# Attention feeding a squared-ReLU MoE: which side of a PSUM copy is strided, and in which order the first loads run

## The chip, the cores and the metric

One core of a Trainium2 chip runs the whole program in one launch. The metric is the device time in microseconds. TensorE (PE) multiplies, VectorE (DVE), ScalarE (ACT) and GpSimd (POOL) work element by element, SyncE (SP) and POOL issue DMAs; all five run their own instruction streams in order and wait for each other by semaphores.

## The reference

Attention over 8 batch rows, 8 heads, 576 positions, head size 64. Heads 0 to 3 see a sliding window of 32 positions, heads 4 to 7 every fourth position of the last 128. The attention output, as 4608 tokens of 512 values, goes through an expansion to 2048, a squared ReLU and a projection back.

```python
rel = pos[:, None] - pos[None, :]
mask_plain = (rel >= 0) & (rel < 32)
mask_dil = (rel >= 0) & (rel < 128) & (rel % 4 == 0)
scores = np.where(masks, scale * (q @ k.T), -1e9)
attn = softmax(scores)
x = (attn @ v).transpose(0, 2, 1, 3).reshape(4608, 512)
h = x @ w_in                  # 512 x 2048
out = np.maximum(h, 0.0) ** 2 @ w_out   # 2048 x 512
```

Inputs and output are float32; the kernel works in fp16 with fp32 sums.

## The kernel before

The program alternates two kinds of work. **Attention** (`attn`) takes one batch row at a time, 8 in all. **MoE** (`moe_gen`) takes chunks of 512 tokens, 9 in all. `moe_gen(c)` is a generator that yields after every two matmuls or so, 64 times in all, and `pump(n)` runs it n yields further. From batch row 1 on, `attn(b, ...)` calls `pump(gap)` between its steps with a gap of 3, so that chunk b-1 fills the holes of row b; what is left of the chunk is pumped at the row's end. After row 7 chunks 7 and 8 run alone.

One row of attention, by the names that profile and text use:

- The loads. q and k of the sliding heads come as fp32 into `sq`, v as fp32 into `sv` (sliding, six DMAs) and `sd` (dilated, two DMAs), all on SP's queue. q and k of the dilated heads come already cast to fp16 into `nd`, on POOL's queue. A DMA from POOL can cast, and the weights `wi` and `wo` (4 DMAs of 512 KB each, counted as fp16) come that way too. `sq`, `sv` and `sd` have one buffer, `nq` and `nd` two.
- Casts: `sq` to `nq`, `sv` to `vp`, `sd` to `vd`. For row 0 DVE casts `nq`, POOL `vp` and ACT `vd`; later rows cast all on POOL.
- `t_sliding` (two calls per row) transposes `nq` on PE into the PSUM tile `pt`, 12 transposes of 96 columns; then DVE copies the half of k and ACT the half of q into `QKTp`. `t_dilated` does the same from `nd` by `pd` to `QKTd`, with two copies on each engine. A row of q was loaded as groups of 6 (or 12) neighbouring positions in one partition, so the transposes leave position 6p+j at column 96j+p, and the copies put the positions in order.
- `s_sliding` and `s_dilated` compute scores into `ps` and `pz`, ACT takes the exponential into `AT`, DVE multiplies by a mask.
- `av_sliding` and `av_dilated` compute `pav` and `paw`; DVE divides by the sum (RECIPROCAL, then x_p or x_d). `x_sliding` and `x_dilated` transpose the result into `px` and `py`, and DVE copies them into `xT`, the input of the MoE.

All these PSUM tiles (pt, pd, ps, pz, pav, paw, px, py) share **two** buffers of one pool: pd can start only when pt's buffer has been emptied by DVE and ACT, the second ps only when pd's has. In a MoE chunk `ph` is the PSUM tile of the expansion (16 per chunk, 4 matmuls each), ACT takes the ReLU (`rt`), DVE squares it (`g`), and `po` is the tile of the projection (4 per chunk, 16 matmuls each), copied by ACT into `ot` and stored by SP. ph and po share four further buffers.

The instruction order on each engine follows the code, with shifts by the Tile framework's scheduler, which moves an instruction ahead where its inputs come earlier; the order within an engine is then fixed. Before the loop the program issues the loads of row 0 and `wi`, then casts, the loads of row 1, the attention of row 0 without any MoE work, and `wo`. L129 and L131 are the lines of `copy`, one helper for all the copies and casts named above: `scalar.copy` on ACT, `tensor_copy` on DVE and POOL.

Of the kernel before, what the change touches and what calls it, by code (L numbers as in the profile page):

```python
# [9 lines left out]
FP32 = mybir.dt.float32  # L10
I16 = mybir.dt.int16
ALU = mybir.AluOpType
ACTF = mybir.ActivationFunctionType
P = 128
# [3 lines left out]
def kernel(  # L18
# [9 lines left out]
    nc = tc.nc  # L28

    B, H, S, D = q.shape  # L30
    W = 32
    DIL = 4
# [13 lines left out]
    QB = 96  # L46
    NB = S // QB
    PADP = P - QB
    CL = S // DIL
    QD = CL // 2  # L50
    PADD = P - QD
    UW = 576

    const = ctx.enter_context(tc.tile_pool(name="const", bufs=1))
# [51 lines left out]
        return nd  # L106

    def load_w_in():
        for j in range(4):
            nc.gpsimd.dma_start(  # L110
                out=wi[:, :, 512 * j : 512 * (j + 1)],
                in_=moe_w_in[:, 512 * j : 512 * (j + 1)].rearrange(
                    "(dh dl) f -> dl dh f", dl=P
                ),
            )

    def load_w_out():
        for j in range(4):
            nc.gpsimd.dma_start(
                out=wo[:, 4 * j : 4 * (j + 1), :],  # L120
                in_=moe_w_out[4 * j * P : 4 * (j + 1) * P, :].rearrange(
                    "(fh fl) m -> fl fh m", fl=P
                ),
            )


    def copy(eng, o, i):
        if eng is nc.scalar:
            nc.scalar.copy(o, i)  # L129
        else:  # L130
            eng.tensor_copy(o, i)  # L131
# [12 lines left out]

    def cast_v(engs):
        for m in range(0, NB, 2):
            copy(engs[0], vp[:, m : m + 2, :, 0:D], sv[:, m : m + 2, :, :])
        for t in range(2):
            for c in range(0, DIL, 2):
                copy(  # L150
                    engs[1],
                    vd[:, t, c : c + 2, :, 0:D],
                    sd[:, t, :, D * c : D * (c + 2)].rearrange("p h (c d) -> p c h d", d=D),
                )
# [4 lines left out]
    nc.vector.memset(sv[0:PADP, 0, :, :], 0.0)  # L159
    nc.vector.memset(sd[0:64, 0, :, :], 0.0)  # L160
    load_v(0)
    load_w_in()

    make_identity(nc, ident)
    reli = const.tile([P, QB], I16, name="reli")
# [33 lines left out]
    def moe_gen(c):  # L199
        g = gp.tile([P, NFF, TOKC], FP16, name=f"g{c}", tag="g")  # L200
        for ffc in range(NFF):
            ph = pmool.tile([P, TOKC], FP32, name=f"ph{c}_{ffc}", tag="pm")
            for dmk in range(NDM):
                nc.tensor.matmul(  # L204
                    ph,
                    wi[:, dmk, ffc * P : ffc * P + P],
                    xT[:, dmk, c * TOKC : (c + 1) * TOKC],
                    start=(dmk == 0),
                    stop=(dmk == NDM - 1),
                )  # L210
                if dmk == 1:
                    yield
            rt = osb.tile([P, TOKC], FP16, name=f"rt{c}_{ffc}", tag="rt")
            nc.scalar.activation(rt, ph[:], ACTF.Relu)  # L214
            nc.vector.tensor_mul(g[:, ffc, :], rt, rt)  # L215
            yield
        for t in range(TOKC // P):
            po = pmool.tile([P, DM], FP32, name=f"po{c}_{t}", tag="pm")
            for ffc in range(NFF):
                nc.tensor.matmul(  # L220
                    po,
                    g[:, ffc, t * P : (t + 1) * P],
                    wo[:, ffc, :],
                    start=(ffc == 0),
                    stop=(ffc == NFF - 1),
                )
# [24 lines left out]
    def t_sliding(b, n, hp):  # L251
        pt = pa(f"pt{b}_{hp}", FP16)
        for i in (1, 0):
            for j in range(6):
                nc.tensor.transpose(  # L255
                    pt[:, i, QB * j : QB * (j + 1)],
                    n[:, i, j, 2 * hp : 2 * hp + 2, :],
                    ident[0:QB, 0:QB],
                )
        for i, eng in ((1, nc.vector), (0, nc.scalar)):  # L260
            copy(
                eng,
                QKTp[:, i, hp, PADP:].rearrange("x (p j) -> x j p", j=6),
                pt[:, i, 0:UW].rearrange("x (j p) -> x j p", p=QB),
            )

    def t_dilated(b, n, g):
        pt = pa(f"pd{b}_{g}", FP16)
        for i in (1, 0):
            for j in range(6):  # L270
                nc.tensor.transpose(  # L271
                    pt[:, i, QB * j : QB * (j + 1)],
                    n[:, i, g, P * j : P * (j + 1)],
                    ident[0:QB, 0:QB],
                )
        for i, eng in ((1, nc.vector), (0, nc.scalar)):
            for h in range(2):
                copy(
                    eng,
                    QKTd[:, i, 2 * g + h, :, PADD:].rearrange("x a (p s) -> x a s p", s=3),  # L280
                    pt[:, i, 0:UW].rearrange("x (s a h p) -> x a h s p", a=2, h=2, p=48)[
                        :, :, h
                    ],
                )
# [99 lines left out]
    def x_dilated(b, t, xs):  # L384
        py = pa(f"py{b}_{t}", FP16)
        for a in range(2):
            for e in range(2):
                x = xs[a][:, e].rearrange("p h d -> p (h d)")
                for c in range(2):
                    o = 288 * c + QD * (2 * a + e)  # L390
                    nc.tensor.transpose(  # L391
                        py[:, 0, o : o + QD],
                        x[0:QD, P * c : P * (c + 1)],
                        ident[0:QD, 0:QD],
                    )
        t0 = b * S + 288 * t
        nc.vector.tensor_copy(  # L397
            xT[:, 2:4, t0 : t0 + 288].rearrange("x c (i r) -> x c r i", r=DIL),
            py[:, 0, 0:UW].rearrange("x (c r i) -> x c r i", c=2, r=DIL),
        )  # L400

    def attn(b, nq, nd, gap):
        t_sliding(b, nq, 0)
        pump(gap)
        t_sliding(b, nq, 1)
        pump(gap)
        t_dilated(b, nd, 0)
        pump(gap)
        s_sliding(b, 0)
        pump(gap)  # L410
        t_dilated(b, nd, 1)
        pump(gap)
        s_sliding(b, 1)
        pump(gap + 2)
        s_dilated(b, 0)
        pump(gap + 2)
        s_dilated(b, 1)
        pump(gap + 1)
        xs = []
        for mp in range(3):  # L420
            xs.append(av_sliding(b, mp))
            pump(gap)
            if mp == 1:
                x_sliding(b, 0, xs)
# [12 lines left out]
        pump(gap)  # L437
        x_dilated(b, 1, zs)

    nq = cast_sliding_qk(0, (nc.vector, nc.vector))  # L440
    cast_v((nc.gpsimd, nc.scalar))
    load_sliding_qk(1)
    load_v(1)
    attn(0, nq, nds[0], 0)
    nds[1] = load_dilated_qk(1)
    load_w_out()
    nxt = 0
    for b in range(1, B):
        pending.append(moe_gen(b - 1))
        pump(1)  # L450
        nq = cast_sliding_qk(b, (nc.gpsimd, nc.gpsimd))
        cast_v((nc.gpsimd, nc.gpsimd))
        if b + 1 < B:
            load_sliding_qk(b + 1)
            load_v(b + 1)
            nds[b + 1] = load_dilated_qk(b + 1)
        attn(b, nq, nds[b], 3)
        pump(1000)
    for c in range(B - 1, NTOKC):
        pending.append(moe_gen(c))  # L460
# [31 lines left out]
```

## Time and profile before

| | |
|---|---|
| time, median of 2 runs | 399.22 us (399.0 to 399.44) |
| the profiled execution's own time | 401.02 us |
| its span, first to last instruction | 399.2 us |
| PE busy | 328.8 us (82%) |
| DVE, ACT, POOL busy | 227.0, 186.4, 80.8 us |
| granted PE clock, mean of the span | 0.970 |
| HBM read and written | 39.85 and 9.44 MB |

Lines of the profile read "line, engine, operation, output <- input, shapes, count", then busy time and mean ns of one, then how long the engine stood idle before the group and what ended the wait. A timeline row has start and length in us first. A stretch row (from:to) has the length, then busy us and count for PE, PE's weight loads, DVE, ACT and POOL, the granted clock, the DMA share and GB/s. A row of a DMA queue has packets, MB and the time of its packets as a share of 16 engines over the stretch.

### The profile page before, as it was taken

Reading aid. Unit: us, or ns where it says so; the run is one execution under the profiler, and the core shown is the slowest. Engines: PE = TensorE matmul, PEld = TensorE weight load, DVE = VectorE, ACT = ScalarE, POOL = GpSimd, SP = SyncE. Lnnn points to the kernel's source line nnn. Section 1 sums busy time; section 2 is a strip of 40 time slices with the busy share of each in tenths; the row PEclk is TensorE's granted clock in tenths of the full one; section 3 lists DMA queues with packets and bytes.
Section 4 is the critical chain, followed back from the end, with each engine's and each line's share of the span. In section 5 each row is a group of like instructions: output and inputs, shape, how many; then the busy total and the mean of one; then the engine's idle time right before and its main releaser. Section 6 shows DMA issues by size and latency. Waiting matters only on the chain.

```text
span 399.2 us, 6698 instructions
## 1 busy us (share of the span) xinstructions
PE 328.8 (82%) x2656; PEld 170.0 (43%) x2656; DVE 227.0 (57%) x420; ACT 186.4 (47%) x297; POOL 80.8 (20%) x127
## 2 busy tenths in 40 slices
PE   0203677999699969996999699969996999999995
PEld 0102443455345524552455345534553455444442
DVE  4603787757575666666665666566666666420410
ACT  0018327812791188218821773178317841642721
POOL 6045045162222132313231322100210000000000
PEclk9999998999899989999899989998999899999999
DMA  8999999978434454445344033400010001001002
GB/s 179 196 219 209 196 221 193 182 161 236 121 59 116 148 120 62 103 162 118 62 103 136 27 59 95 145 27 2 29 53 28 0 13 69 26 27 68 12 29 80
DMA packets 50368, 40.81 MB, mean 102 GB/s; under 512 B 26016, under 2 KB 45728, under 8 KB 50336
## 3 DMA queue, kind: packets, MB, share of 16 engines
q1 hardware_dynamic: 42528, 31.46, 32.2%
q0 software_dynamic: 7808, 8.92, 13.8%
q8 instruction: 21, 0.34, 0.3%
q14 instruction: 11, 0.09, 0.1%
HBM read 39.85 MB, written 9.44 MB: 123 GB/s over the span
## 4 chain that ended last, share of the span: by engine, by line
PE 68%; ACT 12%; DVE 11%; DMA 5%; issue 2%; SPq 0%; ACTq 0%
PE po L220 31%; PE ph L204 26%; ACT QKTp L129 6%; DVE QKTp L131 4%; DMA sd<-in_v_dram 3%; ACT QKTd L129 3%; DVE QKTd L131 2%; ACT rt L214 2%; PE pd L271 2%; PE paw L358 2%; DMA sq<-in_k_dram 2%; PE pav L344 1%; PE pz L315 1%; PE ps L297 1%; DVE g L215 1%
## 5 line engine op out<-in xcount | busy, mean ns | idle before, releaser
L204 PE MATMUL ph<-xT,wi 128*128 128x512 f16 x576 | 149.2, 400 | 0.1
L220 PE MATMUL po<-wo,g 128*128 128x512 f16 x576 | 137.2, 379 | 0.0
L214 ACT ACTIVATE rt<-ph 128x512 f16<-128x512 f32 x144 | 87.6, 624 | 42.6 <-PE ph L204 42.2
L215 DVE TENSOR_TENSOR g<-rt 128x512 f16<-128x512 f16 x144 | 67.0, 465 | 66.3 <-ACT rt L214 63.7
L230 ACT COPY ot<-po 128x512 f32<-128x512 f32 x36 | 21.1, 586 | 121.6 <-PE po L220 118.2
L204 PEld LDWEIGHTS <-wi 128*128 128x128 f16 x576 | 52.9, 102 | 56.6 <-issue 7.4
L220 PEld LDWEIGHTS <-g 128*128 128x128 f16 x576 | 51.7, 98 | 51.7
L271 PE MATMUL pd<-ident,nd 96*128 96x96 f16 x192 | 14.9, 246 | 31.0 <-ACT QKTp L129 30.4
L131 DVE COPY QKTp<-pt 128x576 f16<-128x576 f16 x16 | 33.0, 2080 | 7.4 <-PE pt L255 7.4
L131 POOL CAST vp<-sv 128x512 f16<-128x512 f32 x24 | 15.3, 641 | 105.8 <-PE pav L344 41.7
L129 ACT COPY QKTp<-pt 128x576 f16<-128x576 f16 x16 | 33.1, 2094 | 7.4 <-DVE QKTp L131 7.4
L131 POOL CAST nq<-sq 96x768 f16<-96x768 f32 x28 | 23.7, 882 | 41.8 <-PE pt L255 27.7
L131 DVE COPY QKTd<-pd 128x288 f16<-128x288 f16 x32 | 18.0, 634 | 22.3 <-PE pd L271 22.2
L271 PEld LDWEIGHTS <-nd 96*128 96x128 f16 x192 | 13.8, 122 | 37.5 <-issue 36.1
L297 PE MATMUL ps<-QKTp 64*128 64x96 f16 x192 | 10.6, 218 | 21.5 <-ACT QKTd L129 15.6
L397 DVE COPY xT<-py 128x576 f16<-128x576 f16 x16 | 23.0, 1443 | 6.1 <-PE py L391 5.3
L131 POOL CAST vd<-sd 128x512 f16<-128x512 f32 x28 | 17.3, 624 | 30.2 <-PE paw L358 27.5
L330 DVE TENSOR_TENSOR x_d<-paw,rcp_d 72x512 f16<-72x512 f32 x32 | 22.0, 686 | 1.1
L297 PEld LDWEIGHTS <-QKTp 64*128 64x128 f16 x192 | 7.2, 99 | 34.2 <-issue 30.8
L129 ACT COPY QKTd<-pd 128x288 f16<-128x288 f16 x32 | 17.9, 661 | 7.6 <-DVE QKTd L131 7.5
L255 PE MATMUL pt<-ident,nq 96*128 96x96 f16 x192 | 11.9, 216 | 10.3 <-DVE nq L131 10.3
L287 ACT ACTIVATE AT<-ps 128x576 f16<-128x576 f32 x32 | 19.2, 652 | 1.6 <-PE ps L297 1.6
(46 smaller groups left out, 218.3 us busy)
## 6 DMA issues: line engine op xcount, KB each, us to landing
out_dram<-ot SPq DMA_DIRECT2D x36, 256.0 KB, 2.9
sv<-in_v_dram SPq DMA_DIRECT2D x40, 128.0 KB, 2.8
sq<-in_q_dram SPq DMA_DIRECT2D x8, 576.0 KB, 8.8
sq<-in_k_dram SPq DMA_DIRECT2D x8, 576.0 KB
sd<-in_v_dram SPq DMA_DIRECT2D x8, 512.0 KB
nd<-in_q_dram POOLq DMA_DIRECT2D x16, 144.0 KB, 5.9
nd<-in_k_dram POOLq DMA_DIRECT2D x16, 144.0 KB, 6.3
sd<-in_v_dram SPq DMA_DIRECT2D x8, 288.0 KB
```

The costliest lines, as they stand in the source:

```text
L129: nc.scalar.copy(o, i)
L131: eng.tensor_copy(o, i)
L204: nc.tensor.matmul(ph, wi[:, dmk, ffc * P : ffc * P + P], xT[:, dmk, c * TOKC : (c + 1) * TOKC], start=(dmk == 0), stop=(dmk == NDM - 1),)
L214: nc.scalar.activation(rt, ph[:], ACTF.Relu)
L215: nc.vector.tensor_mul(g[:, ffc, :], rt, rt)
L220: nc.tensor.matmul(po, g[:, ffc, t * P : (t + 1) * P], wo[:, ffc, :], start=(ffc == 0), stop=(ffc == NFF - 1),)
L230: nc.scalar.copy(ot, po)
L271: nc.tensor.transpose(pt[:, i, QB * j : QB * (j + 1)], n[:, i, g, P * j : P * (j + 1)], ident[0:QB, 0:QB],)
L287: nc.scalar.activation(AT[:, u, 0:UW], ps[:, :, 0 : UW // 2], ACTF.Exp, scale=scale)
L297: nc.tensor.matmul(ps[:, e, QB * m3 : QB * (m3 + 1)], QKTp[r, 1, hp, QB * m : QB * m + P], QKTp[r, 0, hp, PADP + QB * m : PADP + QB * (m + ...
L330: nc.vector.tensor_tensor(out=x[0:w], in0=pv[:, :, :, 0:D], in1=rcp[0:w].unsqueeze(3).to_broadcast([w, 2, HH, D]), op=ALU.mult,)
L397: nc.vector.tensor_copy(xT[:, 2:4, t0 : t0 + 288].rearrange("x c (i r) -> x c r i", r=DIL), py[:, 0, 0:UW].rearrange("x (c r i) -> x c r i ...
```

## The change

Two things are changed. The first is the access pattern of the copies that reorder positions: QKTp from pt, QKTd from pd, and xT from py. Before, they read PSUM in its order and write fp16 with a step of 6, 3 and 4 elements; now they read PSUM with a step of 96, 192 and 72 elements and write in order.

```diff
-                QKTp[:, i, hp, PADP:].rearrange("x (p j) -> x j p", j=6),
-                pt[:, i, 0:UW].rearrange("x (j p) -> x j p", p=QB),
+                QKTp[:, i, hp, PADP:].rearrange("x (p j) -> x p j", j=6),
+                pt[:, i, 0:UW].rearrange("x (j p) -> x p j", j=6),
...
-                    QKTd[:, i, 2 * g + h, :, PADD:].rearrange("x a (p s) -> x a s p", s=3),
-                    pt[:, i, 0:UW].rearrange("x (s a h p) -> x a h s p", a=2, h=2, p=48)[
+                    QKTd[:, i, 2 * g + h, :, PADD:].rearrange("x a (p s) -> x a p s", s=3),
+                    pt[:, i, 0:UW].rearrange("x (s a h p) -> x a h p s", a=2, h=2, p=48)[
...
-            xT[:, 2:4, t0 : t0 + 288].rearrange("x c (i r) -> x c r i", r=DIL),
-            py[:, 0, 0:UW].rearrange("x (c r i) -> x c r i", c=2, r=DIL),
+            xT[:, 2:4, t0 : t0 + 288].rearrange("x c (i r) -> x c i r", r=DIL),
+            py[:, 0, 0:UW].rearrange("x (c r i) -> x c i r", c=2, r=DIL),
```

The second is the start of the program. wi is issued (in three DMAs, the last of double size) only behind the vp casts of row 0, wo behind the vd casts, and the loads of row 1 stand in the code behind three small memsets into sq, sv and sd. For row 0 ACT and DVE cast one half of nq each and POOL casts vp and vd. ACT gets a first activation of one column, which loads its table. Chunk 0 starts before row 1's attention, which then runs with a gap of 1.

```diff
     load_v(0)
-    load_w_in()
+    warm = const.tile([P, 1], FP32, name="warm")
+    nc.vector.memset(warm, 0.0)
+    nc.scalar.activation(warm, warm, ACTF.Exp)
...
-    nq = cast_sliding_qk(0, (nc.vector, nc.vector))
-    cast_v((nc.gpsimd, nc.scalar))
+    nq = cast_sliding_qk(0, (nc.scalar, nc.vector))
+    cast_v_sliding()
+    load_w_in()
+    cast_v_dilated()
+    load_w_out()
+    attn(0, nq, nds[0], 0)
+    pending.append(moe_gen(0))
+    pump(1)
+    pump(14)
+
+    nc.vector.memset(sq[:, :, :, 0:1], 0.0)
+    nc.vector.memset(sv[:, 1, :, 0:1], 0.0)
+    nc.vector.memset(sd[:, 1, :, 0:1], 0.0)
     load_sliding_qk(1)
     load_v(1)
-    attn(0, nq, nds[0], 0)
     nds[1] = load_dilated_qk(1)
-    load_w_out()
+    pump(18)
     for b in range(1, B):
-        pending.append(moe_gen(b - 1))
-        pump(1)
+        if b > 1:
+            pending.append(moe_gen(b - 1))
+            pump(1)
...
-        attn(b, nq, nds[b], 3)
+        attn(b, nq, nds[b], 1 if b == 1 else 3)
```

POOL's first casts and DMAs, before (nd_98 is row 0's nd, nd_433 row 1's, nq_446 row 1's nq):

```order
L105 DMA nd_98<-in_q_dram 48x2x768 x2
L105 DMA nd_98<-in_k_dram 48x2x768 x2
L110 DMA wi<-in_moe_w_in_dram 128x4x512 x4
L131 CAST vp<-sv 128x8x64 x3
L105 DMA nd_433<-in_q_dram 48x2x768 x2
L105 DMA nd_433<-in_k_dram 48x2x768 x2
L119 DMA wo<-in_moe_w_out_dram 128x4x512 x4
L131 CAST nq_446<-sq 96x768 x4
```

and after the change (nd_502 and nq_579 are row 1's):

```order
L105 DMA nd_98<-in_q_dram 48x2x768 x2
L105 DMA nd_98<-in_k_dram 48x2x768 x2
L145 CAST vp<-sv 128x8x64 x3
L110 DMA wi<-in_moe_w_in_dram 128x4x512 x2
L110 DMA wi<-in_moe_w_in_dram 128x4x1024
L150 CAST vd<-sd 128x8x64 x4
L117 DMA wo<-in_moe_w_out_dram 128x4x512 x4
L105 DMA nd_502<-in_q_dram 48x2x768 x2
L105 DMA nd_502<-in_k_dram 48x2x768 x2
L129 CAST nq_579<-sq 96x768 x4
```

wi has moved behind the casts of v, and the nd of row 1 has moved behind wo on the same queue.

DVE around the first transposes of row 0, before (nq_140 is row 0's nq, pt_0 and pt_1 its two pt):

```order
L131 CAST nq_140<-sq 96x768 x4
L168 CAST relf<-reli 128x96
L178 TENSOR_TENSOR maskp<-lo__125,hi__126 128x576
L178 TENSOR_TENSOR maskd<-lo__125,hi__126 128x576
L131 COPY QKTp<-pt_0_162 128x6x96
L131 COPY QKTp<-pt_1_177 128x6x96
```

and after:

```order
L129 CAST nq_139<-sq 96x768 x2
L451 MEMSET sq 96x8
L169 CAST relf<-reli 128x96
L179 TENSOR_TENSOR maskp<-lo__124,hi__125 128x576
L452 MEMSET sv 128x4
L179 TENSOR_TENSOR maskd<-lo__124,hi__125 128x576
L129 COPY QKTp<-pt_0_158 128x576
L129 COPY QKTp<-pt_1_173 128x576
```

The scheduler has put two of the three memsets ahead of the copies that empty pt; the third, on sd, stands between the maskp and the maskd products of row 0. The one on sv follows the first vp cast, the one on sd the third vd cast.

ACT where row 1's attention begins, before (rt_0 to rt_3 belong to chunk 0, pt_0 and pt_1 to row 1):

```order
L214 ACTIVATE rt_0_490<-ph_0_443 128x512
L129 COPY QKTp<-pt_0_473 128x6x96
L214 ACTIVATE rt_1_498<-ph_1_493 128x512
L214 ACTIVATE rt_2_521<-ph_2_516 128x512
L129 COPY QKTp<-pt_1_501 128x6x96
```

and after:

```order
L215 ACTIVATE rt_14_565<-ph_14_560 128x512
L215 ACTIVATE rt_15_573<-ph_15_568 128x512
L127 COPY QKTp<-pt_0_606 128x576
L127 COPY QKTp<-pt_1_623 128x576
L288 ACTIVATE AT<-ps_0_0_659 128x576
```

All 16 ph of chunk 0 now stand ahead of row 1's first transposes, and row 1 is mixed with the po of chunk 0. From row 2 on the order on PE, ACT and DVE is nearly that of before.

More of the change, by code (lines that the diff above doesn't have):

```diff
@@ L108, in load_w_in @@
     def load_w_in():
-        for j in range(4):
+        for f0, f1 in ((0, 512), (512, 1024), (1024, 2048)):
             nc.gpsimd.dma_start(
[L111 to L114, printed above, removed]
+                out=wi[:, :, f0:f1],
+                in_=moe_w_in[:, f0:f1].rearrange("(dh dl) f -> dl dh f", dl=P),
             )
@@ L143, in cast_sliding_qk, with cast_v_sliding, cast_v_dilated @@
         return n
-    def cast_v(engs):
+    def cast_v_sliding():
         for m in range(0, NB, 2):
-            copy(engs[0], vp[:, m : m + 2, :, 0:D], sv[:, m : m + 2, :, :])
+            nc.gpsimd.tensor_copy(vp[:, m : m + 2, :, 0:D], sv[:, m : m + 2, :, :])
+    def cast_v_dilated():
         for t in range(2):
             for c in range(0, DIL, 2):
-                copy(
-                    engs[1],
+                nc.gpsimd.tensor_copy(
                     vd[:, t, c : c + 2, :, 0:D],
@@ L438, in attn @@
         x_dilated(b, 1, zs)
-    nq = cast_sliding_qk(0, (nc.vector, nc.vector))
-    cast_v((nc.gpsimd, nc.scalar))
+    nq = cast_sliding_qk(0, (nc.scalar, nc.vector))
[10 more added lines that the diff above has]
+    nc.vector.memset(sd[:, 1, :, 0:1], 0.0)
     load_sliding_qk(1)
     load_v(1)
-    attn(0, nq, nds[0], 0)
     nds[1] = load_dilated_qk(1)
-    load_w_out()
-    nxt = 0
+    pump(18)
     for b in range(1, B):
-        pending.append(moe_gen(b - 1))
-        pump(1)
+        if b > 1:
+            pending.append(moe_gen(b - 1))
+            pump(1)
         nq = cast_sliding_qk(b, (nc.gpsimd, nc.gpsimd))
-        cast_v((nc.gpsimd, nc.gpsimd))
+        cast_v_sliding()
+        cast_v_dilated()
         if b + 1 < B:
```

## The prediction

> **What bounds the kernel now.** I read the page's shares first, then stretches cut where the chain of waits changes its character, then the chain itself.
>
> ```profile
> span 399.2 us, 6698 instructions
> ...
> PE 328.8 (82%) x2656; PEld 170.0 (43%) x2656; DVE 227.0 (57%) x420; ACT 186.4 (47%) x297; POOL 80.8 (20%) x127
> ```
> ```profile
> 0.00:33.60 33.60, 2.29 (x24) 1.94 (x25) 11.15 (x22) 5.44 (x7) 13.68 (x27) 1.00 1.09 200
> 54.90:95.80 40.90, 35.52 (x310) 18.62 (x309) 28.97 (x49) 20.66 (x33) 18.01 (x28) 0.96 1.00 191
> 95.80:136.50 40.70, 36.66 (x317) 19.11 (x316) 26.71 (x48) 21.28 (x34) 10.06 (x15) 0.96 0.47 121
> ```
> TensorE (PE, first number after the length) bounds the whole, but unevenly. In the first 33.6 us it works 2.3 us while the DMA engines (last two numbers: share, GB/s) are full. From 54.9 us each batch row costs some 40.8 us, with about 4 us of PE idle and a mean clock of 0.96.
>
> ```profile
> 94.06 1.73 PE po L220 x8
> ...
> 134.82 1.73 PE po L220 x8
> ...
> 339.73 13.81 PE ph L204 x64
> ...
> 381.17 13.83 PE po L220 x64
> ```
> The chain repeats itself: 134.82 - 94.06 = 40.76 us a row. At the end, with no attention left, 64 matmuls take 13.81 us, 0.216 us each, so a chunk of MoE is 27.6 us. That part can't shrink; the other 13.1 us of a row can. Row 4's PE and one copy, in the timeline:
>
> ```profile
> 180.35 2.10 ACT L129 COPY QKTp<-pt 128x576 f16<-128x576 f16 x1 [1.09 <-DVE QKTp L131]
> 182.50 0.67 PE L271 MATMUL pd<-ident,nd 96*128 96x96 f16 x12 [1.20 <-ACT QKTp L129]
> 184.90 0.30 PE L297 MATMUL ps<-QKTp 64*128 64x96 f16 x6 [0.43 <-ACT QKTp L129]
> 187.96 0.30 PE L297 MATMUL ps<-QKTp 64*128 64x96 f16 x6 [2.22 <-ACT QKTd L129]
> 188.19 1.82 PE L204 MATMUL ph<-xT,wi 128*128 128x512 f16 x4
> 189.81 1.17 PE L271 MATMUL pd<-ident,nd 96*128 96x96 f16 x12
> 190.77 1.93 PE L204 MATMUL ph<-xT,wi 128*128 128x512 f16 x6
> 192.63 0.30 PE L297 MATMUL ps<-QKTp 64*128 64x96 f16 x6
> ```
> PE waits 1.20 + 0.43 + 2.22 = 3.85 us, always for the copy that empties the PSUM buffer it wants next. Then it runs slow: the 4 ph take 1.62 us to the next start instead of 4 x 0.216 = 0.86, the 12 pd 1.17 against the 0.67 of 182.50, the 6 ph 1.86 instead of 1.30. That is 1.8 us more, behind the longest wait alone, where the granted clock falls. Together a row loses **5.6 us** here.
>
> **The copies.** Groups of instructions (mean ns of one before the second bar):
>
> ```profile
> L131 DVE COPY QKTp<-pt 128x576 f16<-128x576 f16 x16 | 33.0, 2080 | 7.4 <-PE pt L255 7.4
> L129 ACT COPY QKTp<-pt 128x576 f16<-128x576 f16 x16 | 33.1, 2094 | 7.4 <-DVE QKTp L131 7.4
> L131 DVE COPY QKTd<-pd 128x288 f16<-128x288 f16 x32 | 18.0, 634 | 22.3 <-PE pd L271 22.2
> L129 ACT COPY QKTd<-pd 128x288 f16<-128x288 f16 x32 | 17.9, 661 | 7.6 <-DVE QKTd L131 7.5
> L397 DVE COPY xT<-py 128x576 f16<-128x576 f16 x16 | 23.0, 1443 | 6.1 <-PE py L391 5.3
> L287 ACT ACTIVATE AT<-ps 128x576 f16<-128x576 f32 x32 | 19.2, 652 | 1.6 <-PE ps L297 1.6
> L330 DVE TENSOR_TENSOR x_p<-pav,rcp_p 96x512 f16<-96x512 f32 x24 | 16.4, 683 | 0.6
> L329 DVE RECIPROCAL rcp_p<-pav 96x8 f32<-96x8 f32 x24 | 4.8, 199 | 7.9 <-PE pav L344 7.9
> L175 DVE TENSOR_SCALAR hi__126<-relf 128x96 f16<-128x96 f32 x1 | 0.2, 203 | 0.0
> L175 DVE TENSOR_SCALAR hi__126<-relf 128x72 f16<-128x72 f32 x1 | 0.2, 190 | 0.0
> ```
> The same 576 elements go from PSUM to contiguous fp16 on ACT in 652 ns (AT<-ps), but to QKTp, whose writes step 12 bytes, in 2094. The steps order the price: 6 bytes (QKTd), 8 (xT from py), 12. So the slow side is the write, and the change takes it away. What the strided read costs, no row shows well. From below: no more than a contiguous read, which on DVE is (683 - 199) / (512 - 8) = 0.96 ns an element over 0.19 us. From above: the RECIPROCAL reads 8 elements 264 bytes apart in 199 ns; the two L175 rows give a fixed part of 203 - 96 x 13 / 24 = 151 ns, so a strided element costs 6.0 ns at most. I take the lower end: in every row above the steps on the write side account for the excess, and x_p, which reads PSUM in broken runs of 64, keeps the plain rate. Then QKTp takes 0.19 + 576 x 0.96 ns = **0.74 us** on DVE and 0.65 on ACT (the AT row), QKTd 0.47 and 0.42 (the same line at 288; for ACT an estimate by its proportion). xT from py falls to 0.74 too; PE has 8 po matmuls to do meanwhile (94.06), so this counts nothing after row 0, and were that cover gone 1.4 us a row.
>
> Row 4 walked again with these numbers. DVE empties pt0 from 178.24 to 178.98; ACT, after its rt, by 179.9; PE wants that buffer for pd0 at 181.1: no wait. pt1 is through both engines by 181.5 and is wanted at 182.9: none. pd0 ends at 181.9; DVE must first do the g of rt2, so its two QKTd copies run 182.4 to 183.3 and ACT's two to 184.1; the second ps wants them at 183.6: **0.5 us** remains, since ACT still starts after DVE. The second pd has the same shape: 0.6. Neither gap is long enough to cost clock (behind the 1.20 us one the 12 pd ran in 0.67). So 1.1 stays of 5.6: **4.5 us a row**, six rows (2 to 7), **27 us**.
>
> **The start.**
>
> ```profile
> 8.85 1.81 DVE L131 CAST nq<-sq 96x768 f16<-96x768 f32 x2 [0.75 <-DMA sq<-in_k_dram]
> ...
> 15.01 0.61 POOL L131 CAST vp<-sv 128x512 f16<-128x512 f32 x1 [7.71 <-DMA sv<-in_v_dram]
> ...
> 28.15 1.28 ACT L129 ACT_TABLE_LOAD   x1 [28.15 <-DMA sd<-in_v_dram]
> ...
> 33.64 1.12 PE L271 MATMUL pd<-ident,nd 96*128 96x96 f16 x12 [21.05 <-ACT QKTp L129]
> ...
> 50.57 1.90 PE L204 MATMUL ph<-xT,wi 128*128 128x512 f16 x4
> ```
> ACT does nothing until sd lands at 28.15, because its first work is the vd casts; its QKTp copies are queued behind, and PE waits for them from 12.6 to 33.64. The vd casts go to POOL and ACT casts q instead (two casts of some 0.9 us from 6.3 on, beside DVE's wait for k, free). DVE's casts of k still end at 10.66, and the transposes near 12.3. The memset on sq is behind them and waits for nothing late. The one on sv stands in DVE's queue **ahead of both QKTp copies** and waits for the first vp cast, now done at 15.6. The DMA queues in two stretches, 12 to 16 us and 28 to 32 us, say how early it can be:
>
> ```profile
> q0 software_dynamic: 624, 0.62, 91.4%
> q1 hardware_dynamic: 631, 0.16, 30.0%
> ```
> ```profile
> q1 hardware_dynamic: 639, 0.92, 108.5%
> q0 software_dynamic: 1, 0.00, 0.2%
> ```
> Beside wi (POOL's queue, q0) the v loads (SP's queue, q1) get packet for packet, 0.16 MB in 4 us; alone q1 moves 0.92. With wi moved behind the vp casts I put the first vp cast's end at 12.5, the last at 14.5, sd at 18 and vd at 20.5. So QKTp is out at 14.8 and pd0 starts there, 19 us sooner. From pd0 to the first ph is 50.57 - 33.64 = 16.9 us; eight QKTd copies on that chain give 1.2 back, so ph begins at 30.5. The memset on sd waits for the third vd cast near 20, the masks that it holds up are due near 23: nothing.
>
> Then the loads. wi is issued at 15; q0 had 1 packet in 28 to 32 although nd was issued at 27, so data flow from 19.5. Its 2.1 MB (four times 512 KB) at 0.62 MB in 4 us are 13.5 us, more while row 1's q and k run beside it: 34.5. The 32 ph up to there are covered by its first half. wo, queued behind, lands at 48, and row 1's nd (four times 144 KB) **behind wo**, at 51.5. PE does its 64 ph by 45.5, then both pt of row 1 and 7 po by 48, and waits 3.5 us for nd. From pd0 on row 1 needs row 0's 16 us, about 2 more for the po between, and 4.5 for py and the last po: chunk 1 starts at **74** instead of 95.8, **21.8 us** sooner. Without the wait it would be 70.5.
>
> Sum: 27 + 21.8 = 48.8. The profiled span of 399.2 becomes 350.4; its own time of 401.02 is 1.8 over that span, and the median of the two runs, 399.22, lies 1.8 below that time, so the median should be **350 us**.
>
> **Rivals.**
>
> *A strided read takes twice the time per element.* For it: no copy here reads PSUM in steps of 144 to 384 bytes, as all of them will. QKTp then takes 0.19 + 576 x 1.92 ns = 1.30 us on DVE and 1.11 on ACT, but QKTd 0.74 and 0.65, longer than the 0.634 of now. The walk gives waits of 2.5 and 1.7 us at the two ps, 4.2 of 5.6; with some clock lost, 1.2 us a row are gained, 7 in all; the start gives 20. 399.2 - 27 = **372 us**. The Trainium skill's page SBUF — State Buffer (section Door 1: The DMA port swizzle) speaks for this: lines of 16 bytes in SBUF that want at least two hits each, of 8 in PSUM, where "any non-contiguous PSUM access pattern significantly slows down matmuls". The write rows above agree with its SBUF half (12-byte steps cost most); of a PSUM read no run here shows it, and by the page the time would be that of this rival.
>
> *The copies gain nothing* (reads as dear as the writes were): the start alone, about 20: **379 us**.
>
> *Row 1's nd and wo take the start back.* The DMA share is still 1.00 in the stretch from 54.9 to 95.8, and row 2's loads press in. If nd lands at 61 instead of 51.5, chunk 1 starts at 83.5: **360 us**, up to 366 if wo is later still.
>
> *Slower than now:* the strided read costs the upper bound, 6.0 ns. QKTp takes 3.6 us on each engine, DVE then ACT: pt0 is out 7.2 us after 178.24, PE wants it after 2.9. The walk gives waits of 4.4, 2.1, 7.6 and 6.4, 20.5 a row, 15 more than now: 6 x 15 = 90 against a start that keeps 10: **480 us**. It decides from about 3.2 ns an element on, where the row's waits reach 9 us, 3.4 more than now, and six rows eat the 20 us of the start. Against it: 8 elements in 199 ns would then all but fill that row.
>
> **How the numbers follow.** Forecast 0.62, double price 0.20, copies gain nothing 0.06, start taken back 0.09, slower 0.03. The forecast's own range is 340 (both 0.5 us waits gone, no wait for nd) to 358. The range for 8 in 10 goes on to the start taken back and the double price: **338 to 375**; the rest is left out. Faster by over 2% (below 391, about what can be told from no change) are all but the last and a tail between: 0.94; same 0.03, slower 0.03.
>
> **What would show it.** QKTp near 0.74 and 0.65 us, QKTd below 0.5; PE's wait of pd for QKTp gone and that of ps for QKTd near 1 us a row; rows of 36.3 us; ACT's first copy before 15 us; pd of row 0 near 15, the first ph near 30, a PE wait for nd near 50, chunk 1 at 74. It is wrong if QKTp stays over 1.2 us, if the memset on sv holds DVE past 16, or if chunk 1 starts after 84.

## The result, and the profile after

The changed kernel takes **355.4 us** (median of two runs, 355.09 to 355.71) against 399.22. The ratio is 0.8902, with a 95% interval of 0.8863 to 0.8942. The profiled execution took 355.09 us, 1.8 more than its span.

The head of the page of the changed kernel, and its groups of copies by shape:

```profile
span 353.3 us, 6704 instructions
...
PE 318.3 (90%) x2656; PEld 164.3 (46%) x2656; DVE 192.2 (54%) x422; ACT 158.9 (45%) x296; POOL 83.2 (24%) x130
```
```profile
L129 DVE COPY QKTp<-pt 128x576 f16<-128x576 f16 x16 | 12.0, 756 | 14.1 <-PE pt L256 14.1
L127 ACT COPY QKTp<-pt 128x576 f16<-128x576 f16 x16 | 10.2, 638 | 11.4 <-DVE QKTp L129 11.3
L129 DVE COPY QKTd<-pd 128x288 f16<-128x288 f16 x32 | 13.0, 448 | 9.2 <-PE pd L272 9.1
L127 ACT COPY QKTd<-pd 128x288 f16<-128x288 f16 x32 | 11.2, 403 | 5.8 <-DVE QKTd L129 5.8
L398 DVE COPY xT<-py 128x576 f16<-128x576 f16 x16 | 12.1, 757 | 9.9 <-PE py L392 9.9
```

DVE and ACT are busy 34.8 and 27.5 us less, PE 10.5 us less, though its number of matmuls is the same: before, it ran part of each row at a lower clock. QKTp went from 2080 and 2094 ns to 756 and 638.

The chain repeats itself in shorter steps, and its end is the old one:

```profile
114.78 1.73 PE po L221 x8
150.43 1.73 PE po L221 x8
...
292.09 1.73 PE po L221 x8
293.81 13.81 PE ph L205 x64
```

Rows 3 to 7 end with the start of the 64 ph: before they took (339.73 - 136.50) / 5 = 40.65 us each, now (293.81 - 116.50) / 5 = 35.46 (116.50 is 114.78 + 1.73, the end of row 2). The stretches of row 2 and row 3, in the columns of the front table's stretch rows:

```profile
78.03:116.50 38.47, 35.61 (x318) 18.41 (x317) 22.83 (x48) 17.58 (x34) 16.30 (x25) 1.00 0.89 217
116.50:152.20 35.70, 35.01 (x318) 18.30 (x316) 22.18 (x48) 17.79 (x34) 10.18 (x15) 1.00 0.52 127
```

Row 3 has PE busy 35.01 of 35.70 us at a full clock. Row 2, which follows the start directly, is 2.8 us longer, with the DMA engines still 0.89 busy. Now PE's timeline, row 0 first, then row 1, the start of chunk 1, two waits of row 2 and the one wait that is left in row 4:

```profile
15.08 1.12 PE L272 MATMUL pd<-ident,nd 96*128 96x96 f16 x12 [2.72 <-ACT QKTp L127]
...
30.15 1.90 PE L205 MATMUL ph<-xT,wi 128*128 128x512 f16 x4
...
57.31 1.12 PE L272 MATMUL pd<-ident,nd 96*128 96x96 f16 x12 [6.85 <-DMA nd<-in_k_dram]
...
78.03 0.59 PE L205 MATMUL ph<-xT,wi 128*128 128x512 f16 x2
...
82.77 0.59 PE L205 MATMUL ph<-xT,wi 128*128 128x512 f16 x2 [0.95 <-ACT ot L231]
...
87.84 0.30 PE L298 MATMUL ps<-QKTp 64*128 64x96 f16 x6 [1.30 <-ACT QKTd L127]
...
159.33 0.30 PE L298 MATMUL ps<-QKTp 64*128 64x96 f16 x6 [0.54 <-ACT QKTd L127]
```

The gain of the span is 45.9 us. Up to the start of chunk 1 it is 95.80 - 78.03 = 17.8 (95.80 is the prediction's mark, the end of chunk 0's last po; chunk 1's first ph began at 95.63); behind it 303.4 becomes 275.3, 28.1: row 2 gives 40.70 - 38.47 = 2.2 and rows 3 to 7 give 5 x 5.19 = 25.9.

### The profile page after: what moved, and what is told of

Same layout as the page of the kernel before. It is cut to its first block, busy times and chain, and to the rows that moved or that the text cites. A ratio compares the mean times of both kernels' runs of the same rounds, so it can differ in the third digit from the quotient of the medians.

```text
span 353.3 us, 6704 instructions
## 1 busy us (share of the span) xinstructions
PE 318.3 (90%) x2656; PEld 164.3 (46%) x2656; DVE 192.2 (54%) x422; ACT 158.9 (45%) x296; POOL 83.2 (24%) x130
## 4 chain that ended last, share of the span: by engine, by line
PE 61%; DMA 16%; ACT 7%; DVE 6%; issue 4%; POOL 2%; SPq 2%; POOLq 0%; ACTq 0%
PE po L221 31%; PE ph L205 22%; DMA sq<-in_k_dram 5%; DMA wi<-in_moe_w_in_dram 4%; DMA sq<-in_q_dram 3%; ACT rt L215 3%; DVE QKTd L129 3%; DVE g L216 2%; DMA sv<-in_v_dram 2%; SPq L92 2%; PE paw L359 2%; DMA out_dram<-ot 2%; ACT QKTd L127 1%; PE pt L256 1%; POOL nq L129 1%
## 5 line engine op out<-in xcount | busy, mean ns | idle before, releaser
L205 PE MATMUL ph<-xT,wi 128*128 128x512 f16 x576 | 139.1, 382 | 2.3 <-ACT rt L215 1.0
L221 PE MATMUL po<-wo,g 128*128 128x512 f16 x576 | 140.1, 381 | 0.0
L129 POOL CAST nq<-sq 96x768 f16<-96x768 f32 x28 | 24.1, 894 | 43.3 <-PE pt L256 20.7
L272 PE MATMUL pd<-ident,nd 96*128 96x96 f16 x192 | 12.1, 219 | 10.2 <-DMA nd<-in_k_dram 6.8
L129 DVE COPY QKTp<-pt 128x576 f16<-128x576 f16 x16 | 12.0, 756 | 14.1 <-PE pt L256 14.1
L288 ACT ACTIVATE AT<-pz 128x576 f16<-128x576 f32 x32 | 19.1, 650 | 0.1
L289 DVE TENSOR_TENSOR AT<-AT,maskp 128x576 f16<-128x576 f16 x32 | 15.0, 468 | 7.5 <-ACT AT L288 5.1
L129 DVE COPY QKTd<-pd 128x288 f16<-128x288 f16 x32 | 13.0, 448 | 9.2 <-PE pd L272 9.1
L398 DVE COPY xT<-py 128x576 f16<-128x576 f16 x16 | 12.1, 757 | 9.9 <-PE py L392 9.9
L256 PEld LDWEIGHTS <-nq 96*128 96x128 f16 x192 | 10.6, 103 | 13.6 <-DVE nq L129 9.6
L289 DVE TENSOR_TENSOR AT<-AT,maskd 128x576 f16<-128x576 f16 x32 | 15.1, 474 | 3.2 <-ACT AT L288 0.3
## 6 DMA issues: line engine op xcount, KB each, us to landing
sq<-in_q_dram SPq DMA_DIRECT2D x8, 576.0 KB, 10.5
```

Source lines behind the costliest of these rows:

```text
L205: nc.tensor.matmul(ph, wi[:, dmk, ffc * P : ffc * P + P], xT[:, dmk, c * TOKC : (c + 1) * TOKC], start=(dmk == 0), stop=(dmk == NDM - 1),)
L221: nc.tensor.matmul(po, g[:, ffc, t * P : (t + 1) * P], wo[:, ffc, :], start=(ffc == 0), stop=(ffc == NFF - 1),)
L256: nc.tensor.transpose(pt[:, i, QB * j : QB * (j + 1)], n[:, i, j, 2 * hp : 2 * hp + 2, :], ident[0:QB, 0:QB],)
L272: nc.tensor.transpose(pt[:, i, QB * j : QB * (j + 1)], n[:, i, g, P * j : P * (j + 1)], ident[0:QB, 0:QB],)
L288: nc.scalar.activation(AT[:, u, 0:UW], ps[:, :, 0 : UW // 2], ACTF.Exp, scale=scale)
L289: nc.vector.tensor_mul(AT[:, u, 0:UW], AT[:, u, 0:UW], mask)
```

## Experiments: the copies

**Each half of the change alone.** First the three new access patterns in the kernel before:

```diff
 # before, start unchanged; QKTp, QKTd and xT as in the change, for example
-                QKTp[:, i, hp, PADP:].rearrange("x (p j) -> x j p", j=6),
-                pt[:, i, 0:UW].rearrange("x (j p) -> x j p", p=QB),
+                QKTp[:, i, hp, PADP:].rearrange("x (p j) -> x p j", j=6),
+                pt[:, i, 0:UW].rearrange("x (j p) -> x p j", j=6),
```

> The three copies of the change in the kernel before, whose start stays. Theory (two separate gains that meet in row 1): rows 2 to 7 give their 28 us, row 1, which here still runs with a gap of 3, some 5, and row 0 some 4, since ACT's two QKTp there end 2.1 us sooner and eight QKTd and two xT copies follow on one chain: 362 us, 358 to 367. Rival (the copies are worth what rows 2 to 7 show and no more, because the start is bound by its loads): 371 us. Rival (half of what rows 2 to 7 gained is owed to the new order at the start): 380 or more.

Measured: 366.2 us (363.9 to 366.4), ratio 0.9167 (0.9134 to 0.9200). The first theory's range holds it, near its upper end: chunk 1 starts at 86.0 and rows 3 to 7 take 35.46 us, but row 2 takes 41.7, with a wait of 4.7 us of ph for ot, which none of the theories had. Then the new start with the three old patterns:

```diff
 # after, start unchanged; QKTp, QKTd and xT as before, for example
-                QKTp[:, i, hp, PADP:].rearrange("x (p j) -> x p j", j=6),
-                pt[:, i, 0:UW].rearrange("x (j p) -> x p j", j=6),
+                QKTp[:, i, hp, PADP:].rearrange("x (p j) -> x j p", j=6),
+                pt[:, i, 0:UW].rearrange("x (j p) -> x j p", p=QB),
```

> The new start with the old copies. Theory: row 0's slow copies hide in the wait for row 1's nd, row 1's rest is some 4 us longer, so chunk 1 starts near 82 and rows take 40.7: 385 us, 380 to 389. Rival (the start is worth its full 17.8 us with any copies): 381. Rival (without fast copies the memsets and ACT's queue hold the start up): chunk 1 after 88, 391 or more.

Measured: 386.1 us (385.6 to 387.8), ratio 0.9686 (0.9650 to 0.9721), as the first theory had it. Chunk 1 starts at 79.7 there, so 16 of the start's 17.8 us come without the fast copies. Against 398.8 the copies alone give 32.6 and the start alone 12.7, together 45.3; both at once gave 43.8. In total the two halves hardly overlap, and the copies carry nearly three quarters. By stage they do overlap: in the profiled executions the copies alone start chunk 1 9.8 us sooner and the new start alone 16.1, where both give 17.8: PE then stands 6.85 us before row 1's nd. Behind that point the copies alone gain 24.9 us (364.5 - 86.0 against 303.4) and the start alone loses 1.5 (384.6 - 79.7), where both gain 28.1; the difference lies in row 2, which is long in each of the two kernels (41.7 and 42.9 us, against 38.5 with both). So the sums agree partly because two differences offset each other.

**One copy at a time**, in the changed kernel:

```diff
 # first run: QKTp stays new, QKTd and xT from py go back, for example
-                    pt[:, i, 0:UW].rearrange("x (s a h p) -> x a h p s", a=2, h=2, p=48)[
+                    pt[:, i, 0:UW].rearrange("x (s a h p) -> x a h s p", a=2, h=2, p=48)[
 # second run: QKTd stays new, QKTp and xT from py go back
```

> The changed kernel with only QKTp copied the new way; QKTd and xT from py as before. Theory (each copy counts by how much later it empties its PSUM buffer): the waits at the two ps return to about 2.8 us a row from 1.3, so 1.5 us a row, 10 in all: 365 us, 362 to 369. Rival (the long QKTp copies were all of it, QKTd is hidden): 357. Rival (xT from py was also on the path): 370 or more.

> The changed kernel with only QKTd copied the new way; QKTp and xT from py as before. Theory: the wait of pd for ACT's QKTp comes back and with it the lower clock, 3 to 3.5 us a row, six rows, and some 2 at the start: 377 us, 373 to 381. Rival (QKTp and QKTd count alike, half of 4.5 us each): 368 to 370. Rival (QKTd counts nothing alone): 382 or more.

Measured: 363.2 us (362.4 to 363.9) and 375.7 us (374.4 to 376.9), both inside the first theory's ranges, ratios 0.9105 (0.9079 to 0.9130) and 0.9418 (0.9388 to 0.9447). PE's waits for copies in row 4, from the timelines: with both old (new start), with QKTp new, with QKTd new.

```profile
168.38 0.67 PE L272 MATMUL pd<-ident,nd 96*128 96x96 f16 x12 [1.20 <-ACT QKTp L127]
170.77 0.30 PE L298 MATMUL ps<-QKTp 64*128 64x96 f16 x6 [0.42 <-ACT QKTp L127]
173.83 0.30 PE L298 MATMUL ps<-QKTp 64*128 64x96 f16 x6 [2.22 <-ACT QKTd L127]
178.47 0.30 PE L298 MATMUL ps<-QKTp 64*128 64x96 f16 x6 [0.78 <-ACT QKTd L127]
```
```profile
163.49 0.30 PE L298 MATMUL ps<-QKTp 64*128 64x96 f16 x6 [1.26 <-ACT QKTd L127]
168.12 0.30 PE L298 MATMUL ps<-QKTp 64*128 64x96 f16 x6 [0.78 <-ACT QKTd L127]
```
```profile
164.21 0.67 PE L272 MATMUL pd<-ident,nd 96*128 96x96 f16 x12 [1.20 <-ACT QKTp L127]
166.60 0.30 PE L298 MATMUL ps<-QKTp 64*128 64x96 f16 x6 [0.42 <-ACT QKTp L127]
168.95 0.30 PE L298 MATMUL ps<-QKTp 64*128 64x96 f16 x6 [1.51 <-ACT QKTd L127]
```

The new QKTp takes away the two waits that name it, and shortens the first wait that names QKTd from 2.22 to 1.26, since the engines come to pd sooner. The new QKTd alone shortens that wait to 1.51, takes away the last one and leaves the other two. From the chain, rows take 40.50, 36.82 and 39.32 us in these three kernels (mean of rows 3 to 7) and 35.46 with both new. A copy counts by how late it gives its PSUM buffer back, not by its own length: DVE and ACT copy a pt one after the other, twice a row, so the new QKTp saves 2 x (1.32 + 1.46) = 5.6 us of copying and gains 3.7 us a row. In the row 4 shown it is the waits that shrink, from 4.62 to 2.04 us, and the row from 39.8 to 37.0, at full clock in both kernels. Most of the rest of the 3.7 is clock: the other four rows with both old copies had a mean clock of 0.96 and took 40.5 to 40.7 us. How long the waits are does not decide this alone. With the new QKTd, rows 4 and 5 wait 3.1 us each at the same three places:

```profile
158.96:197.43 38.47, 35.20 (x318) 18.37 (x316) 26.02 (x48) 20.39 (x34) 10.12 (x15) 1.00 0.48 114
197.43:237.32 39.89, 36.77 (x317) 19.06 (x316) 26.21 (x48) 20.50 (x34) 10.12 (x15) 0.96 0.33 82
```

What decides between the two clocks stays open. What xT from py is worth by itself was not tried.

**What the strided read still costs.** The same copies without any stride:

```diff
-                QKTp[:, i, hp, PADP:].rearrange("x (p j) -> x p j", j=6),
-                pt[:, i, 0:UW].rearrange("x (j p) -> x p j", j=6),
+                QKTp[:, i, hp, PADP:],
+                pt[:, i, 0:UW],
 # and likewise QKTd and xT from py
```

> The changed kernel with QKTp, QKTd and xT from py copied without any stride, read and write both in order; this leaves the reordering of positions out, so its time is that of copies with no strided side. Theory (the strided read costs ACT nothing and DVE only the doubled rate that it has on contiguous fp16): ACT 0.64 and 0.40 as now, DVE's QKTp 0.46 instead of 0.756, QKTd near 0.3; DVE hands over 0.3 us earlier, so the waits at the ps shrink from 1.0 to 0.4 a row: 351 us, 349 to 354. Rival (the strided read still costs both engines twice what it must): ACT's QKTp below 0.5 and 345 or less. Rival (nothing is hidden there any more, the rows are bound by PE alone): 355.

Measured: 350.8 us (349.7 to 351.5), ratio 0.8775 (0.8721 to 0.8830), the first theory. Groups, and the stretch of one row:

```profile
L129 DVE COPY QKTp<-pt 128x576 f16<-128x576 f16 x16 | 7.2, 457 | 16.4 <-PE pt L256 16.4
L127 ACT COPY QKTp<-pt 128x576 f16<-128x576 f16 x16 | 10.1, 638 | 8.8 <-DVE QKTp L129 8.7
L129 DVE COPY QKTd<-pd 128x288 f16<-128x288 f16 x32 | 8.2, 298 | 11.2 <-PE pd L272 11.1
L127 ACT COPY QKTd<-pd 128x288 f16<-128x288 f16 x32 | 11.2, 404 | 9.9 <-DVE QKTd L129 9.9
```
```profile
149.19:184.01 34.82, 34.82 (x317) 18.26 (x316) 20.86 (x48) 17.78 (x34) 10.16 (x15) 1.00 0.51 126
```

ACT takes 638 and 404 ns with a strided read and without. DVE takes (457 - 298) / 288 = 0.55 ns an element in order and (756 - 448) / 288 = 1.07 with a stride. So the stride on the read side halves DVE's rate and leaves ACT's alone. The rate of a copy without strides stood in the profile before, in xT from px:

```profile
L379 DVE COPY xT<-px 128x576 f16<-128x576 f16 x16 | 7.3, 458 | 7.3 <-PE px L373 7.3
```

With no stride at all a row is PE's 34.82 us without a gap, which is the floor for this order of work. The changed kernel is 0.6 us a row above it.

## Experiments: the start

The prediction had PE wait 3.5 us for row 1's nd; it waited 6.85, since nd came at 57.3 instead of 51.5. The DMA queues between 36 and 40 us and between 44 and 48 us, with wo on q0 in both, show why:

```profile
q0 software_dynamic: 638, 0.64, 93.6%
q1 hardware_dynamic: 607, 0.15, 28.8%
```
```profile
q0 software_dynamic: 498, 0.49, 72.5%
q1 hardware_dynamic: 495, 0.49, 44.7%
```

wo (q0) got 0.64 MB in 4 us beside q1's packets of some 250 bytes (0.15 MB in 607), but 0.49 beside packets of some 1000 bytes (0.49 MB in 495), when SP had come to sd of row 1 and sq of row 2. The two queues shared the engines packet for packet in both stretches, and what q0 got in bytes then depended on the size of the other's packets.

**Row 1's nd ahead of wo**, with three buffers for the output tile ot as before, and with six. The pool `osb` also holds rt, the tile of the ReLU, under a tag of its own, so each run "with six" has six buffers for rt as well; no run separates the two.

```diff
     cast_v_dilated()
+    nds[1] = load_dilated_qk(1)
     load_w_out()
...
-    nds[1] = load_dilated_qk(1)
# second run, also:
-    osb = ctx.enter_context(tc.tile_pool(name="osb", bufs=3))
+    osb = ctx.enter_context(tc.tile_pool(name="osb", bufs=6))
```

> The changed kernel with row 1's nd issued ahead of wo on POOL's queue. Theory (the 6.85 us wait for nd is a matter of its place behind wo): nd lands near 41, wo near 57, but row 1's transposes and scores fill PE until the last quarter of wo is wanted; chunk 1 starts at 71 to 75 instead of 78: 350 us, 348 to 353. Rival (all these bytes must come in anyway, and the wait moves to po, which then waits for wo): 354 to 356.

Measured: 355.2 us (353.9 to 355.9), ratio 0.8891 (0.8843 to 0.8939): the rival's number, but not for the rival's reason alone. Waits and timeline of this kernel (PE, then ACT's copy of the first ot, then SP's queue):

```profile
PE ph L205 <- ACT ot L231: 5.2, 1, 5.2
...
PE po L221 <- DMA wo<-in_moe_w_out_dram: 2.5, 1, 2.5
```
```profile
74.56 0.59 PE L205 MATMUL ph<-xT,wi 128*128 128x512 f16 x2
...
83.56 1.01 PE L205 MATMUL ph<-xT,wi 128*128 128x512 f16 x2 [5.22 <-ACT ot L231]
```
```profile
57.96 0.58 ACT L231 COPY ot<-po 128x512 f32<-128x512 f32 x1
```
```profile
64.13 2.00 SPq L83 DMA_DIRECT2D sq<-in_k_dram  x1
76.72 0.31 SPq L83 DMA_DIRECT2D sq<-in_q_dram  x1
77.13 0.43 SPq L232 DMA_DIRECT2D out_dram<-ot  x1
```

nd is waited for no longer, and chunk 1 starts at 74.56, 3.5 us sooner. Then row 2 loses it: the first ot is copied at 58.0, but its store leaves SP only at 77.13, behind a load of sq that waits for that buffer's casts. The fourth ot finds no buffer, ACT stands still with it, and ph waits 5.22 us. With six buffers that wait should have gone:

> Row 1's nd ahead of wo, and six buffers instead of three for ot (the output tiles). Theory (with nd early, chunk 1 began 3.5 us sooner, and the gain went into a 5.2 us wait of ph for the fourth ot, whose buffer came free only when the store of the first ot left SP's queue, where it stood behind a load of sq): the wait goes, chunk 1 starts near 74.5 as in the run with three buffers: 350 us, 348 to 352. Rival (the DMA engines, not the buffer, hold the store): no change, 355. Rival (SP's order holds row 3 back as well): 353.

Measured: 355.5 us (355.4 to 356.1), ratio 0.8934 (0.8919 to 0.8949). The theory missed. The wait for ot did go, and chunk 1 started at 75.45, but another came into its place (DVE, POOL and PE, 78 to 88 us; ps is in row 2):

```profile
78.88 0.83 POOL L129 CAST nq<-sq 96x768 f16<-96x768 f32 x1
...
79.39 6.22 DVE L216 TENSOR_TENSOR g<-rt 128x512 f16<-128x512 f16 x2
...
82.08 2.28 POOL L150 CAST vd<-sd 128x512 f16<-128x512 f32 x4
84.32 1.97 POOL L129 CAST nq<-sq 96x768 f16<-96x768 f32 x2
85.53 0.81 DVE L129 COPY QKTd<-pd 128x288 f16<-128x288 f16 x2
...
87.18 0.42 PE L298 MATMUL ps<-QKTp 64*128 64x96 f16 x6 [4.93 <-ACT QKTd L127]
```

Two g, whose median is 0.42 us in this trace, take 6.22 us (the first alone 5.26) while POOL casts row 3's data without a pause; DVE's QKTd copies, ACT's behind them and the second ps follow 5 us late. With three buffers ACT had stood still just then and DVE had no g to do, so this stayed unseen in row 2. The changed kernel has such a g too, of 3.82 us at 36.3, beside the casts of row 1, where PE's wait for nd hides it.

The Trainium skill's page SBUF — State Buffer (section SBUF: two separate sides) has a rule that fits: a DVE instruction with two SBUF inputs and a GpSimd instruction that reads SBUF share a pair of ports, and whichever "starts first gets the pair for the whole instruction". The traces agree in which instructions suffer. In the eight kernels that have all the new copies and the new start, a g takes 0.43 us on average away from POOL's casts and 0.68 beside them, and AT by maskp, which also reads two SBUF tiles, 0.46 and 0.84. Instructions that read PSUM take the same in both cases: QKTp from pt 0.756 and 0.754 us, x_d 0.687 and 0.687. The long g, though, lasted through nine casts in a row, not one. No run took the casts off POOL, so that they are the cause is read from the traces and not isolated.

**Row 2's sq later as well**, with three and with six buffers for ot:

```diff
 # nd ahead of wo, and ahead of the loads of row 2:
+        if b == 1:
+            for i in range(2):
+                nc.vector.tensor_copy(sq[:, i, 0, 0:1], gs[0][0:QB, 15, 0:1])
```

(gs[0] is chunk 0's g; the write makes the load of sq wait for it.)

> As the run before, and row 2's sq is loaded only behind chunk 0's last g, so that its large packets do not share the DMA engines with wo. Theory (packets are dealt one for one, and large ones of row 2 took bandwidth from wo between 38 and 45): wo some 2 to 3 us earlier, chunk 1 at 70 to 73: 349 us, 346 to 351. Rival (row 2's q and k then come too late): a wait of its pt for nq, 353 or more. Rival (wo was not waited for): as the run before.

> Row 1's nd ahead of wo, row 2's sq behind chunk 0, and six buffers for ot. Theory (with three buffers no wait for ot was left here): as that run, 349.8 us, 348 to 351. Rival (the copies into ot hold up ACT elsewhere, unseen as a wait of PE): 347 or less.

Measured: 349.8 us (348.8 to 352.2), ratio 0.8768 (0.8712 to 0.8824), and 350.2 us (349.6 to 351.7), ratio 0.8802 (0.8776 to 0.8827). The first theory's ranges hold. These are the fastest of the kernels that keep the reordering of positions, some 5 us below the changed one. Chunk 1 started at 72.1 and 75.1; the first profiled execution was the fastest of its four and the second the slowest, so these 3 us may be no difference of the kernels. Row 2 took 38.1 us in both, about as in the changed kernel: POOL's casts are spread there by waits for the later sq, and the longest two g beside them took 2.62 us with three buffers for ot, where the run before had 6.22. A later sq without the earlier nd was not run.

**What the change at the start lives on.** First wi back ahead of the casts of v, without the memsets, and with three and six buffers for ot; then row 0's vd casts back on ACT:

```diff
 # first and second run
     load_v(0)
+    load_w_in()
...
     cast_v_sliding()
-    load_w_in()
     cast_v_dilated()
 # third run, in place of cast_v_dilated() for row 0
-                nc.gpsimd.tensor_copy(
+                nc.scalar.copy(
```

> The changed kernel with wi issued right behind row 0's loads, before the casts of v, as in the kernel before, and without the three memsets (the scheduler would else put one of them ahead of the first copies on DVE). Theory (the loads of row 0, row 1 and both weights must all be in before row 1 can go on, and their sum sets the time, not the place of wi): v comes late again, sd near 28, so the first ph comes near 37 instead of 30, but nd of row 1 lands by 54 to 57 as now: chunk 1 at 75 to 79, 353 to 357 us. Rival (the late v delays row 0 and with it all that follows): chunk 1 after 83, 361 or more.

> wi ahead of the casts of v, no memsets, and six buffers for ot. Theory (with three buffers chunk 1 began at 76.9, a little before the changed kernel's 78.0, and the whole loss was an 8.4 us wait for the fourth ot): 352 us, 350 to 354, so wi's place is worth nothing or less. Rival (late v and row 0 cost what the three-buffer run lost): 359 to 361.

> The changed kernel with row 0's vd casts on ACT again, ahead of its QKTp copies, and six buffers for ot. Theory (the loads of weights and of row 1 set the start, row 0's chain has slack against them): pd of row 0 starts near 21 instead of 15, the first ph near 36 instead of 30, but PE still stands before nd at 57 and chunk 1 still starts near 78; without the 1 us wait for ot 354.5 us, 353 to 356. Rival (row 0's chain sets the start, as the prediction had it for most of the 21.8 us): 6 us later, 360 to 361.

Measured: 360.5 us (360.0 to 361.2), ratio 0.9027 (0.8981 to 0.9074); 353.2 us (352.3 to 355.5), ratio 0.8864 (0.8842 to 0.8886); 355.2 us (352.9 to 356.4), ratio 0.8916 (0.8874 to 0.8958). The first came near the rival's number with the theory's mechanism: chunk 1 began at 76.9, before the changed kernel's 78.0, and an 8.4 us wait for the fourth ot followed. Six buffers gave some 7 us back, about as the theory had it. The third kept to the theory too; its timeline on PE:

```profile
20.22 1.12 PE L272 MATMUL pd<-ident,nd 96*128 96x96 f16 x12 [8.14 <-ACT QKTp L127]
...
35.20 1.90 PE L205 MATMUL ph<-xT,wi 128*128 128x512 f16 x4
...
55.34 0.67 PE L272 MATMUL pd<-ident,nd 96*128 96x96 f16 x12 [1.22 <-DMA nd<-in_k_dram]
...
75.92 0.59 PE L205 MATMUL ph<-xT,wi 128*128 128x512 f16 x2
```

Row 0 runs 5 us later here, and chunk 1 starts 2 us sooner than in the changed kernel. Row 0's chain has that much slack, because row 1 can't go on before its own loads are in: the wait for nd is 1.22 us here and 6.85 in the changed kernel. The changed kernel was not run with six buffers, so its fair partner is missing; its own wait for ot was 0.95 us, which leaves the rival's 6 us ruled out, but not a cost of 1 or 2 us.

The start of chunk 1, and the time from there to the end of chunk 1's last po (row 2), worked out from the timelines and the chain, one execution each (executions of one kernel differ by 0.6 to 3.5 us in all). The last column is what row 2 takes beyond the mean of rows 3 to 7 of the same kernel:

| kernel | chunk 1 starts | row 2 takes | beyond rows 3 to 7 |
|---|---|---|---|
| changed | 78.0 | 38.5 | 3.0 |
| copies only | 86.0 | 41.7 | 6.2 |
| start only | 79.7 | 42.9 | 2.4 |
| nd ahead of wo; with six ot | 74.6; 75.5 | 42.8; 42.2 | 7.3; 6.7 |
| and row 2's sq late; with six ot | 72.1; 75.1 | 38.1; 38.1 | 2.7; 2.6 |
| wi first; with six ot | 76.9; 76.6 | 45.4; 40.7 | 9.9; 5.2 |
| vd on ACT, six ot | 75.9 | 40.0 | 4.5 |

Except where row 2's sq comes late, what is won ahead of chunk 1 against the changed kernel is given back in row 2 wholly or for the greater part, where SP's stores, POOL's casts of row 3 and PE meet. Waits are not all of it: the mean clock of row 2 was 1.00 in the changed kernel and in the two with a late sq, and 0.92 to 0.96 in all the others of the table. With the new copies, row 2 less PE's waits is 35.4 to 35.8 us in the former and 36.5 to 37.6 in the latter.

## Why the prediction was right, and where it was off

- **Prices of the copies: right, on DVE by luck in part.** 0.74, 0.65, 0.47, 0.42 and 0.74 us were forecast, and 0.756, 0.638, 0.448, 0.403 and 0.757 measured. The argument took DVE's 0.96 ns an element from rows with fp32 sources and called it the price of a contiguous read. For fp16 the profile of before had a contiguous copy out of PSUM, at 458 ns for 576 elements, which the prediction did not use (the row of xT from px, above). Beside this row the strided fp16 read does cost DVE about twice per element, 1.07 against 0.55 ns, as the first rival said; it was forecast well because the fp32 rate lies close to that. On ACT the rival's factor does not exist. The rule of the Trainium skill that was weighed there (SBUF — State Buffer, section Door 1: The DMA port swizzle) speaks of matmuls and gives no price, so the rival's 372 was not its figure; ACT's 638 ns with and without stride speaks against it for ACT's copies, and for matmuls no run here shows it.
- **Row waits: right, a little too small.** 4.5 us a row were forecast and 5.2 came in rows 3 to 7. One wait of 0.5 stayed, the second pd's of 0.6 did not. The clock was 1.00 through the row, as said. Row 2 gave only 2.2, and rows 3 to 7 made up for it, so six rows came to 28.1 against 27.
- **Row 0: right.** pd at 15.08 (14.8 forecast), first ph at 30.15 (30.5). The memset on sv did stand ahead of the QKTp copies: without the memsets pd began at 13.6, though wi stood first in those runs too; and the run with vd on ACT shows that row 0 has about 5 us to spare.
- **Chunk 1's start: a term mis-sized.** 74 was forecast, 78.0 measured. The step that failed is that wo "lands at 48", and row 1's nd behind it "at 51.5": the rate of 0.62 MB in 4 us was taken from a stretch where the other queue carried small packets, and it fell to 0.49 beside larger ones. wi landed at 35.8 (34.5 forecast), wo at 51.3 and nd at 57.2, so the 2.7 MB of wo and nd took 21.4 us, 0.50 MB in 4 us, where 17 had been allowed. nd was thus 5.7 us late; chunk 1 was only 4.0 late, because row 1 took 20.7 us from its pd on where 22.5 were forecast. Those 4.0, against 1.1 more from the rows, make the span 353.3 instead of 350.4.
- **The credit of the start: partly wrong.** The 19 us that pd0 gains are real, but a row 0 with 5 us less of that gain, or wi in its old place, came out at 355.2 and 353.2 us with six buffers, against the changed kernel's 355.4 with three. With three buffers wi in its old place cost 5 us, in the wait for ot. That before it took both together (v late behind wi, and ACT held by v's casts) to make row 0 late enough to matter is an inference; no run with the new start has both. Chunk 0 ahead of row 1's attention, row 1's gap of 1 and its earlier loads stand in every run with the new start, so which of them carries the start's gain was not tried and stays open.
- **What comes late next was not followed into row 2.** The prediction treated it as a row like the others. It took 2.8 us more than row 3, with waits of 0.95 us for ot, 0.44 for QKTp and 1.30 for QKTd; the experiments show what the first and the last can grow to. "Without the wait it would be 70.5" was half right: with nd ahead of wo chunk 1 started at 74.6, then with 2.5 us of waiting for wo, and the time stayed.
- **From span to median: wrong by 2.1 us.** The profiled execution of before lay 1.8 above the median of its runs, and the same was assumed of after. There the median, 355.4, lies 2.1 above the span. The excess of the execution time over the span (1.8) carries over; that the one profiled execution lay above the median does not. This and the 2.9 us of the span make the 5 us between 350.4 and 355.4.

## What to carry to other kernels

Where a copy out of PSUM reorders fp16 elements as these do, put the stride on the read side and write in order; its price shows in the wait for the PSUM buffer that it empties, so walk the next user of that buffer. At a start that is bound by loads, moving one load ahead of another moves the wait; the row behind the start has to be walked too, because it inherits the queues. A store that stands behind a load in one queue waits for whatever that load's buffer waits for.

## What the runs showed of the hardware

A write of 2-byte elements with a step of 6, 8 or 12 bytes cost 634, 1443 and 2080 ns on DVE (288, 576 and 576 elements). With the write in order, PSUM reads with steps of 192 and 384 bytes cost ACT nothing (638 and 403 ns, against 638 and 404 without a stride), and steps of 144 to 384 bytes cost DVE 0.5 ns an element. A g of 0.42 us took 5.26 us beside dense casts of POOL, while DVE's copies out of PSUM kept their length beside them. And the DMA queues shared by packets, so that the same queue got 0.64 or 0.49 MB in 4 us.
